# Feed-forward chunks of 384 tokens instead of 256 in the later two thirds of a fused attention and feed-forward kernel

## The chip, the cores and the metric

The kernel runs on one core of a Trainium2 chip. The metric is the device time of one execution in microseconds (us). The kernel before took 922.78 us, the median of three runs (922.3 to 923.05).

## The reference

Eight batches of eight heads, 576 tokens and 64 values per head; all is float32. For each head two attentions are added. One is over tokens averaged in fours (144 of them) and its result is repeated four times. The other is local: a token sees only those less than four positions away, seven at most. The sum is read as 4608 rows of 512 values and goes through a feed-forward layer with a leaky ReLU.

```
q_d, k_d, v_d = means over 4 neighbouring tokens
out = repeat(softmax(q_d k_d^T / 8) v_d, 4) + softmax(q k^T / 8, |i-j| < 4) v
x   = out as (4608, 512)
h   = x @ w_in                       # (512, 2048)
g   = max(h, 0) + alpha * min(h, 0)
y   = g @ w_out                      # (2048, 512)
```

## The kernel before, in words

**Precision.** Weights, x and g are each held as a high and a low part of a four-byte format, so each product of the feed-forward is three matmul groups: high by high, low weight by high operand, high weight by low operand.

**The feed-forward (scope `s`).** The 4608 tokens are 18 chunks of 256 (`T`). A chunk takes 8 steps, 144 in all (`NS`), and a step treats two blocks of 128 of the 2048 hidden values:

- `hidden(s)` (L987): for both blocks 12 matmuls on TensorE (PE): 3 part groups x 4 slices of the 512 inputs, weights 128x128, moving operand x of 256 columns, into one PSUM bank `h` (two of these, 128x512).
- `below(s)` (L993): ScalarE (ACT) writes relu(-h) into the SBUF tile `t`.
- `leak(s)` (L1009): VectorE (DVE) forms t * rise + h, once for each block.
- `split(s)` (L1015): ACT copies the high part `gh`; `spill(s)` (L1021): GpSimd (POOL) subtracts for the low part `gl`. `t`, `gh`, `gl` have two buffers each.
- `product(s)` (L1049): 2 blocks x 3 part groups x 2 output blocks of 128 tokens, 12 matmuls of 512 columns into the two banks `o` of the chunk. The step order on PE is hidden(s), product(s-2), hidden(s+1), product(s-1).
- After a chunk's last step `stage` (L1056) copies each bank `o` to an SBUF tile on ACT and `send` (L1062) writes it out in four transfers on SyncE's queue (SP). `finish_last` does so for the last chunk, with ACT and DVE copies and transfers on both queues.

**The operand of a chunk** is a tile `xx` of 2 (token parity) x 2 (high, low) x 4 x 128 values per partition. There are three buffers, two in pool `two` and one in pool `late`; chunk c takes them in turn (`operand`, `tokens`).

**Attention.** Batch 0 is computed first with matmuls (scopes `p0` to `p3`). From batch 1 on, a *unit* u (3 to 23, `local`) is the local attention of 192 rows of x, so three units make a batch. DVE multiplies keys with the query (`multiply`, L821), sums (`total`, L825), masks (`shift`, L834), normalises (`weights`) and weighs the values (`first`, `weigh`, `gather`, `last`); POOL takes the two farthest keys (`far`, L863). ACT copies the query of each half unit into a PSUM bank first (`scaled`, L815): in most units the first half into bank q and the second into bank l, where the sums also live. In units of `BY_HALF` the two halves run one after the other. Scope `d` (28 of these, four per batch) is the attention over averaged tokens: POOL folds the loads, PE does the matmuls, DVE and ACT the softmax.

When a unit is done, PE transposes it (`flip`, L891), DVE adds the averaged part (`join`, L903, into tile `xf`, one buffer), ACT writes the high operand into `xx` (`place`, L917) and POOL the low one (L208). This happens inside the time of the next unit, in two groups of tokens (`put`).

**The order of the work.** Every action is an event with a time in steps: hidden(s) at s - 1.95, leak(s) at s - 1.15, product(s) at s + 0.6, unit u from `begin[u]` to `begin[u+1]`. `begin` is a table (`UNITS`) and then rises by `U_STEP` = 5.92. Events are issued in the order of their times, and each engine and queue takes its instructions in that order. For the first 42 steps (`HORIZON`) a list written out by hand or by a planner (`ORDER`, 1193 names) replaces the times.

**Weights** are loaded from 0 to some 100 us (`raw`, L289 and L293), and decoded into high and low parts by ACT and DVE.

The changed functions: `tokens`, `spans`, `local`, `hidden`, `below`, `leak`, `split`, `spill`, `product`, `stage`, `send`, `finish_last`, and new ones `third`, `block`, `pieces`, `moving`, `like`.

Of the kernel before, what the change touches and what calls it, by code (L numbers as in the profile page):

```python
# [52 lines left out]
p2.load1 p0.shift0 p0.flip p0.near1 p0.operands p0.near_exps0 p2.load3 p0.shift1 p0.scores p1.turned00 p0.near_exps1
p0.weights i0.convert p1.turn04 p1.turn10 p1.turned04 p1.turned10 i0.bits p1.turn14 p0.load3 p0.over1 p1.turned14
p0.peak o0.convert p1.near0 p1.fold0 p0.exps p1.fold1 o1.load i0.upper p0.invert p2.turn00 i1.load p1.shift0 p1.flip
p0.scaled p0.over0 i0.lower p1.load2 p1.near_exps0 p0.across0 p1.operands p3.load0 o0.bits p0.kept0 p0.across1
p0.held0 p1.near1 p0.kept1 p3.load1 p0.held1 o0.upper p0.over2 p1.shift1 p0.weigh p0.kept2 o0.lower p2.turned00
p0.near_weigh0 d10.load.0 p1.near_exps1 p0.store d10.load.1 p1.weights d10.load.3 p0.near_weigh1 p3.load3 p2.turn10
p0.join0 p2.turn04 p0.high0 p2.turned10 p0.low0 p0.near_weigh2 p2.turned04 p1.scores p2.fold0 p0.join2 p0.join1
i1.convert p2.turn14 p1.load3 p1.peak p1.over0 p2.fold1 p2.turned14 p1.exps p1.over1 p1.fold_v i2.load p2.near1  # L60
i1.bits p2.load2 p1.kept0 p1.kept1 p1.invert p1.over2 o1.convert o2.load p2.near0 i1.upper d10.fold.0 p3.load2
d10.fold.1 p0.high1 p1.scaled p0.low1 d10.load.4 i1.lower p3.turn00 d10.load.2 p1.kept2 p2.flip p3.turned00
# [10 lines left out]
i5.load i4.convert p3.near_weigh1 d10.fold.5 d10.operands p3.near_weigh0 d11.fold.0 d11.load.2 o3.upper d10.scores
d11.load.3 p3.join0 o3.lower p3.high0 p3.low0 p3.near_weigh2 d11.fold.1 s.hidden.0 d10.peak p3.join1 d10.exps
i4.bits d11.load.4 p3.high1 p3.join2 o5.load d10.invert i4.upper p3.low1 change o6a.clear w.load_raw.0.6 d10.scale
i4.lower d11.fold.2 s.hidden.1 w.load_q.3 s.below.0 i5b.convert s.leak.0 i5a.convert i5b.bits d11.fold.4
w.load_kv.3.v s.split.0 d10.turn.0 i5a.bits i5b.upper s.hidden.2 w.load_raw.0.7 s.below.1 d10.turned.0 w.load_kv.3.k
s.leak.1 i5a.upper s.spill.0 o4.convert i5b.lower s.hidden.3 i5a.lower d11.fold.3 s.below.2 o4.bits s.split.1
d11.load.5 s.leak.2 i6a.convert d10.turn.1 s.spill.1 d12.load.0 s.product.0 d10.turned.1 d12.load.1 i6a.bits
o4.upper o6b.clear s.below.3 o4.lower w.load_raw.1.6 i6a.upper i6b.convert s.hidden.4 i6a.lower s.split.2 i6b.bits  # L80
s.spill.2 s.leak.3 i6b.upper w.load_raw.1.6~1 d10.weigh i6b.lower d11.flip i7a.convert s.product.1 d11.operands
i7a.bits i7b.convert i7a.upper i7b.bits o5a.convert s.hidden.5 d11.fold.5 i7a.lower w.load_raw.1.7 s.split.3
i7b.upper o5a.bits s.spill.3 o5b.convert d12.load.2 s.below.4 s.product.2 i7b.lower o5a.upper s.leak.4 o6a.convert
d12.fold.0 o5b.bits s.below.5 o6b.convert s.hidden.6 s.leak.5 s.split.4 d12.fold.1 d12.load.3 o5b.upper o5a.lower
d10.store o5b.lower s.spill.4 o6a.bits s.product.3 d12.fold.2 s.below.6 d12.load.4 s.leak.6 o6a.upper o6b.bits
o7a.clear d11.scores d12.load.5 s.split.5 d12.fold.3 o7a.convert s.product.4 o6a.lower o6b.upper d11.peak o7b.clear
o6b.lower d13.load.0 d11.exps s.spill.5 o7a.bits s.hidden.7 o7b.convert d12.fold.4 s.split.6 d11.invert o7b.bits
d11.scale o7a.upper s.hidden.8 s.below.7 o7a.lower s.spill.6 d13.load.1 o7b.upper s.leak.7 u3.scaled.0
w.place_rest.0 d12.fold.5 o7b.lower u3.multiply.0.0.3 d11.turn.0 u3.scaled.1 d11.turn.1 w.place_rest.1 d11.turned.0
s.product.5 d11.turned.1 s.below.8 u3.multiply.0.3.2 s.leak.8 u3.total.0.3.2 d11.weigh s.split.7 u3.total.0.0.3  # L90
d12.flip d11.store s.spill.7 u3.load_q.4 s.product.6 d12.operands u3.multiply.0.5.2 d13.fold.0 u3.multiply.1.0.3
d13.fold.1 d13.load.2 d12.scores s.split.8 u3.total.0.5.2 d13.load.3 s.spill.8 s.product.7 u3.total.1.0.3 d12.peak
u4.scaled.0 u3.multiply.1.3.2 d13.fold.2 d12.exps s.hidden.9 u3.multiply.1.5.2 d13.load.4 s.stage.0.0 u3.total.1.3.2
s.stage.0.1 d13.load.5 u3.total.1.5.2 s.send.0.1 s.product.8 s.below.9 d13.fold.3 d12.invert u3.shift d12.scale
u3.load_kv.4.k d13.fold.4 s.leak.9 u3.exps u3.weights d12.turn.0 s.split.9 d13.fold.5 d12.turn.1 s.hidden.10
d12.turned.0 d12.turned.1 u3.first.0 u3.far.0 u3.weigh.0.1.3 u3.weigh.0.4.1 u3.gather.0.1.0 s.hidden.11 s.below.10
u3.gather.0.1.1 s.spill.9 s.leak.10 u3.far.1 u3.gather.0.1.2 s.split.10 u3.gather.0.4.0 s.hidden.12 s.below.11
u3.weigh.1.1.3 u3.weigh.1.4.1 s.spill.10 s.leak.11 d20.load.0 s.product.9 d20.load.1 u3.last.0 d20.load.2 s.below.12
u3.first.1 s.leak.12 u3.gather.1.1.0 d13.flip s.split.11 s.product.10 u3.gather.1.1.1 d13.operands s.spill.11
u3.gather.1.1.2 d20.fold.0 u3.gather.1.4.0 u4.multiply.0.0.3 d20.fold.1 d12.weigh s.split.12 d13.scores d12.store  # L100
u4.multiply.0.3.2 s.spill.12 s.product.11 u4.total.0.0.3 u3.load_kv.4.v d13.peak d20.load.3 u4.multiply.0.5.2
d13.exps s.hidden.13 d20.fold.2 u3.last.1 u4.total.0.5.2 d20.load.4 u4.scaled.1 d13.invert u4.total.0.3.2 d13.scale
u4.load_q.5 s.product.12 u4.multiply.1.0.3 s.below.13 s.send.0.0 d20.fold.3 u4.multiply.1.3.2 u4.total.1.0.3
d20.fold.4 d13.turn.0 d20.load.5 d13.turn.1 d13.turned.0 s.hidden.14 u4.total.1.3.2 d13.turned.1 d21.load.0
u4.multiply.1.5.2 s.leak.13 u4.total.1.5.2 d13.weigh s.split.13 u4.load_kv.5.k d20.fold.5 u3.flip.0 s.below.14
u4.shift d13.store s.hidden.15 s.leak.14 s.spill.13 u4.exps u3.join.0 s.split.14 s.spill.14 u4.weights u3.place.0.0
u3.flip.1 d20.flip s.below.15 u3.place.0.1 u4.weigh.0.1.3 s.product.13 d20.operands d21.fold.0 u4.weigh.0.4.1
u3.join.1 u4.far.0 s.leak.15 u3.place.1.0 d20.scores d21.load.1 u4.first.0 s.split.15 s.product.14 d20.peak
d21.load.2 u4.gather.0.1.0 d20.exps d21.load.3 u3.place.1.1 u4.gather.0.1.1 u4.gather.0.1.2 s.spill.15 d20.invert
u4.weigh.1.1.3 s.hidden.16 d20.scale u4.far.1 u4.gather.0.4.0 u4.last.0 u4.weigh.1.4.1 s.product.15 s.below.16  # L110
u4.first.1 d21.fold.1 s.leak.16 u4.load_kv.5.v u4.gather.1.1.0 d21.fold.2 s.split.16 d21.load.4 u4.gather.1.1.1
# [1137 lines left out]
```

## Time and profile before

| | |
|---|---|
| median of three runs | 922.78 us |
| the profiled execution | 925.19 us, span 923.4 us |
| PE busy | 900.0 us (97%) |
| DVE busy | 774.3 us (84%) |
| POOL busy | 543.5 us (59%) |
| ACT busy | 420.7 us (46%) |
| granted TensorE clock, mean | 0.975 |
| moved to and from memory | 98.27 MB |

The page shows one execution. The span runs from the first instruction to the last; the profiled execution's own time also holds what lies around it, 1.8 us. Busy time of PE counts a matmul to its modelled end, so that overlapping matmuls look like one long piece; how far the starts lie apart says how fast they go. Lines are grouped by the source line, engine, operation and tiles; after the bar stands the idle time of the engine just before these instructions and what ended it. In the slices a digit is the busy share in tenths of one fortieth of the span, 23.1 us. `h` is the bank of the hidden values, `o` the output bank, `xx` the operand, `wih`, `wil`, `woh`, `wol` the high and low weights.

### The profile page before, as it was taken

To read this page: it belongs to the slowest core of one execution; us is meant where nothing else is said; L and a number is where in the kernel's file an instruction comes from. 1 tells how busy PE (TensorE), PEld (TensorE's weight loads), DVE (VectorE), ACT (ScalarE), POOL (GpSimd) and SP (SyncE) were. 2 spreads that over 40 slices of the span, in tenths; PEclk is the share of its full clock that TensorE was granted. 3 is DMA by queue.
4 is the path that set the end of the run, shared out by engine and by line. 5 is a ranking of instruction groups with operands and counts; after the bars stand their busy time and mean duration, and the time that the engine had idled before them with its cause. 6 is when DMAs were issued, how large, how long until landed. Compare 5 with 4: busy or idle time off the path is not lost.

```text
span 923.4 us, 17740 instructions
## 1 busy us (share of the span) xinstructions
PE 900.0 (97%) x6474; PEld 828.2 (90%) x6474; DVE 774.3 (84%) x1387; ACT 420.7 (46%) x1061; POOL 543.5 (59%) x683
## 2 busy tenths in 40 slices
PE   6799999999999999999999999999999999999998
PEld 5579999999988999999999999999999999999997
DVE  5787899999999499889999889899998899996111
ACT  4798854544444444344444444344444452233221
POOL 2126775886486665748767566867757753426221
PEclk9757999999999999999999999999999999999999
DMA  8997533334334113333133234233334222211000
GB/s 186 220 308 267 175 108 126 104 100 119 114 109 131 60 54 112 97 119 113 61 115 123 79 102 128 72 115 123 85 114 125 65 76 70 74 35 25 1 23 23
DMA packets 63195, 98.27 MB, mean 106 GB/s; under 512 B 23556, under 2 KB 28932, under 8 KB 63108
## 3 DMA queue, kind: packets, MB, share of 16 engines
q1 hardware_dynamic: 62916, 96.88, 35.3%
q8 instruction: 51, 0.84, 0.4%
q10 hardware_dynamic: 192, 0.26, 0.1%
q14 instruction: 36, 0.29, 0.1%
HBM read 87.67 MB, written 9.44 MB: 105 GB/s over the span
## 4 chain that ended last, share of the span: by engine, by line
PE 77%; DVE 12%; DMA 3%; SPq 2%; ACT 2%; issue 1%; POOL 1%; ACTq 0%; DVEq 0%; POOLq 0%
PE h L987 35%; PE o L1049 34%; DMA raw<-in_moe_w_in 3%; DVE qk L821 3%; DVE ls L825 2%; PE s L409 2%; DVE t L1009 2%; PE pv L443 2%; SPq L513 2%; DVE lb L882 2%; DVE pv L879 1%; PE pT L433 1%; PE xp L891 1%; PE qkT L396 1%; DVE xf L903 1%
## 5 line engine op out<-in xcount | busy, mean ns | idle before, releaser
L987 PE MATMUL h<-xx,wih 128*128 128x256 f32 x2304 | 332.6, 278 | 1.6 <-DVE t L1009 1.6
L1021 POOL TENSOR_TENSOR gl<-t,gh 128x512 fp32r<-128x512 f32 x142 | 182.1, 1282 | 241.6 <-ACT gh L1015 227.4
L987 PEld LDWEIGHTS h<-xx,wih 128*128 128x128 f32 x2304 | 299.0, 193 | 8.1 <-DVE t L1009 1.2
L1009 DVE SCALAR_TENSOR_TENSOR t<-t,rise,h 128x256 f32<-128x256 f32 x288 | 124.7, 474 | 73.6 <-ACT t L993 73.2
L1049 PE MATMUL o<-woh,gh 128*128 128x512 f32 x576 | 184.5, 391 | 0.5 <-ACT sg L1056 0.5
L1049 PE MATMUL o<-woh,gl 128*128 128x512 f32 x576 | 177.7, 379 | 0.0
L1049 PE MATMUL o<-wol,gh 128*128 128x512 f32 x576 | 177.7, 379 | 0.0
L987 PE MATMUL h<-xx,wil 128*128 128x256 f32 x1152 | 176.4, 276 | 0.0
L1015 ACT CAST gh<-t 128x512 fp32r<-128x512 f32 x144 | 89.5, 621 | 177.8 <-PE o L1049 88.9
L387 POOL TENSOR_TENSOR ld<-ld 72x256 f32<-72x256 f32 x167 | 125.4, 751 | 69.3 <-DMA ld<-in_q 35.0
L993 ACT ACTIVATE t<-h 128x512 f32<-128x512 f32 x144 | 86.0, 597 | 160.6 <-PE h L987 128.3
L987 PEld LDWEIGHTS h<-xx,wil 128*128 128x128 f32 x1152 | 152.4, 193 | 0.0
L825 DVE TENSOR_REDUCE ls<-qk 128x12 f32<-128x768 f32 (+1 forms) x126 | 135.4, 1081 | 2.3
L1049 PEld LDWEIGHTS o<-woh,gl 128*128 128x128 f32 x576 | 109.1, 189 | 15.3
L1049 PEld LDWEIGHTS o<-wol,gh 128*128 128x128 f32 x576 | 109.1, 189 | 14.8
L1049 PEld LDWEIGHTS o<-woh,gh 128*128 128x128 f32 x576 | 99.8, 190 | 11.2 <-issue 2.2
L882 DVE TENSOR_TENSOR lb<-lb,pv 128x384 f32<-128x384 f32 x168 | 94.7, 564 | 4.5
L821 DVE TENSOR_TENSOR qk<-k,qp 128x768 f32<-128x768 f32 (+1 forms) x78 | 83.3, 1076 | 5.0 <-ACT qp L815 5.0
L879 DVE TENSOR_TENSOR pv<-v,lb 128x1152 f32<-128x1152 f32 x84 | 79.3, 952 | 2.3
L821 DVE TENSOR_TENSOR qk<-k,lb 128x768 f32<-128x768 f32 (+1 forms) x48 | 51.5, 1078 | 1.5 <-ACT lb L815 1.5
L208 POOL TENSOR_TENSOR xx<-xf,xx 128x256 fp32r<-128x256 f32 (+3 forms) x47 | 43.7, 936 | 13.8 <-ACT xx L917 13.8
L903 DVE TENSOR_TENSOR xf<-xp,od 128x128 f32<-128x128 f32 (+3 forms) x110 | 40.0, 415 | 7.5 <-PE xp L891 5.0
(146 smaller groups left out, 997.2 us busy)
## 6 DMA issues: line engine op xcount, KB each, us to landing
v<-in_v SPq DMA_DIRECT2D x41, 384.0 KB
k<-in_k SPq DMA_DIRECT2D x41, 384.0 KB
out<-sg SPq DMA_DIRECT2D x140, 64.0 KB
raw<-in_moe_w_in SPq DMA_DIRECT2D x16, 512.0 KB
raw<-in_moe_w_out SPq DMA_DIRECT2D x16, 512.0 KB
ld<-in_q SPq DMA_DIRECT2D x56, 144.0 KB
ld<-in_k SPq DMA_DIRECT2D x56, 144.0 KB
ld<-in_v SPq DMA_DIRECT2D x56, 144.0 KB
```

Source lines behind the costliest of these rows:

```text
L387: e.tensor_tensor(lv[:, :, 0:128], lv[:, :, 0:128], lv[:, :, 128:256], op=ALU.add)
L821: nc.vector.tensor_tensor(st["qk", half, d0][:, :nd], window(tiles[u, "k"], half, d0, nd), st["qp", half].unsqueeze(1).to_broadcast([128, ...
L825: nc.vector.tensor_reduce(out=st["s"][:, half, d0:d0 + nd, :].rearrange("p a b -> p (a b)"), in_=st.pop(("qk", half, d0))[:, :nd].rearrang ...
L879: nc.vector.tensor_tensor(st["pv", half, d0][:, :nd], window4(tiles[u, "v"], half, d0, nd), prob(half, d0, nd), op=ALU.mult)
L882: nc.vector.tensor_tensor(st["acc"], st["acc"], st["pv", half, d0][:, i], op=ALU.add)
L903: nc.vector.tensor_tensor(xf.rearrange("p a t (s e) -> p e t a s", e=2)[:, par, k0:k0 + nk], tp.rearrange("p (t s e a) -> p e t a s", t=4, ...
L987: nc.tensor.matmul(ph[:, j], w[:, m, 128 * o:128 * o + 128], x[:, part, m], start=(i == 0), stop=(i == 11))
L993: nc.scalar.activation(t, hs[st], AF.Relu, scale=-1.0)
L1009: nc.vector.scalar_tensor_tensor(t[:, j], t[:, j], rise[:, f:f + 1], h[:, j], op0=ALU.mult, op1=ALU.add)
L1015: nc.scalar.copy(gh, t)
L1021: (nc.vector if f"s{st}.split" in ON_VECTOR else nc.gpsimd).tensor_tensor(gl, t, f32(gh), op=ALU.subtract)
L1049: nc.tensor.matmul(outs[c][m], g[:, j, 128 * m:128 * m + 128], wo[w][n][:, :, o].rearrange("p e a -> p a e"), start=(f == 0 and i == 0), s ...
```

## The change

The first six chunks (`SMALL`, 48 steps) stay as they are. The other 3072 tokens become eight chunks of 384. Such a chunk takes 16 steps of one block of 128 hidden values each, with a `PACE` of 0.75 of an old step: 12 matmuls of 384 columns into the first 384 columns of a bank `h`, elementwise work on 128x384, and 9 output matmuls (3 part groups x 3 output blocks). There are 48 + 128 = 176 steps on the same time scale of 144. `leak`, `split` and `spill` are planned 0.2 of a step later.

A chunk's operand takes one and a half of the three old buffers (`A`, `B`, `C`; C has 384 values more): even large chunks use all of A and the first three blocks of B, odd ones all of C and the last two blocks of B, as `pieces` lists. High and low parts are blocks of 192 values per parity, so a low part is written with two or three instructions where it was one.

The third output block uses PSUM bank q (`bank("q", ...)`) and is staged through the tile of the joins, `xf`. So from unit 11 on (`SINGLE`) attention leaves bank q alone: the query is copied to bank l only, first one half and later the other, and the very first multiply of a unit reads the query in SBUF. Outputs of large chunks leave in transfers of up to 128 rows, the first block's on ACT's queue. Units 13, 17 and 21 are no longer done by halves, `UNITS` goes up to 12 with units 9 to 12 earlier than before, then `U_STEP` is 5.96, and the second join of odd units from 9 on comes earlier. The written-out order is a new one of 1507 names, up to step 56, which also orders the first 48 steps anew. The branch of `below` and `leak` for POOL, which was not in use, goes.

```diff
+SMALL = 6
+SIZES = [256] * SMALL + [384] * ((B * S - 256 * SMALL) // 384)
+STARTS = [sum(SIZES[:c]) for c in range(len(SIZES))]
+STEPS = [(c, f, 2 if n == 256 else 1) for c, n in enumerate(SIZES) for f in range(0, NF, 2 if n == 256 else 1)]
+PACE = [1.0 if n == 2 else 0.75 for _, _, n in STEPS]
+WHEN = [sum(PACE[:s]) for s in range(len(STEPS))]
+SINGLE = 11
-UNITS = {3: 7.5, 4: 12.2, 5: 17.07, 6: 22.7, 7: 28.0}
-U_STEP = 5.92
-BY_HALF = (5, 9, 13, 17, 21)
+UNITS = {3: 7.5, 4: 12.2, 5: 17.07, 6: 22.7, 7: 28.0, 8: 33.8, 9: 39.1, 10: 44.4, 11: 50.0, 12: 55.6}
+U_STEP = 5.96
+BY_HALF = (5, 9)
-HORIZON = 42
+HORIZON = 56
...
+    def third(name):
+        if name not in shared:
+            shared[name] = (late if name == "C" else two).tile([128, 2432 if name == "C" else 2048], F32R, tag="xx", name=f"xx{name}")
+        return shared[name]
+
+    def block(name, k, n=1):
+        if k == 5:
+            return third(name)[:, 2048:2432].rearrange("p (m e a) -> p m e a", m=1, e=2)
+        return third(name)[:, 0:2048].rearrange("p (e x) -> p e x", e=2)[:, :, 192 * k:192 * (k + n)]             .rearrange("p e (m a) -> p m e a", m=n)
+
+    def pieces(c, i):
+        if c % 2 == 0:
+            return (("A", 0, 0, 4),) if i == 0 else (("A", 4, 0, 1), ("B", 0, 1, 4))
+        return (("C", 0, 0, 4),) if i == 0 else (("C", 4, 0, 1), ("C", 5, 1, 2), ("B", 3, 2, 4))
+
+    def moving(c, i, m):
+        if c < SMALL:
+            return xT[c].rearrange("p e i m a -> p i m a e")[:, i, m]
+        (x, k), = ((x, f + m - a) for x, f, a, z in pieces(c - SMALL, i) if a <= m < z)
+        return block(x, k)[:, 0].rearrange("p e a -> p a e")
...
+                if single:
+                    st["qp", 0] = st["qp", 1] = lb[:, 0:384].rearrange("p (h n) -> p h n", h=2)
...
+            if single and (half, d0) == (0, 0):
+                q_ = tiles[u, "q"][:, :, 0:3, :].rearrange("p h t d -> p h (t d)")
+            else:
+                q_ = st["qp", half]
...
-                hi, lo = (tokens(c, i, o, n) for i in range(2))
+                    for ms, lo in tokens(c, 1, o, n):
+                        sub(lo, pairs(src[:, ms]), f32(hi[:, :, ms]))
...
+        c, f0, nf = STEPS[st]
+        nm = SIZES[c] // 128
+        if f0 == 0:
+            outs[c] = [ps_o.tile([128, DM], F32, tag="po", name=f"o{c}_{m}") if m < 2 else bank("q", f"o{c}_{m}")
+                       for m in range(nm)]
...
+        if m < 2:
+            sg = two.tile([128, DM], F32, tag="stage", name=f"sg{c}_{m}", bufs=SB)
+        else:
+            sg = late.tile([128, DM], F32, tag="xf", name=f"sg{c}_{m}")
...
+        if c >= SMALL:
+            o = 0
+            for n, ap in rows(STARTS[c] + 128 * m, 128):
+                (nc.scalar if m == 0 else nc.sync).dma_start(ap, sg[o:o + n, :])
+                o += n
+            return
...
+        slip = 0.2 * (nf == 1)
+        at(t - (1.15 - slip) * p, leak, s)
+        at(t - (1.0 - slip) * p, split, s)
+        at(t - (0.99 - slip) * p, spill, s)
...
-            t = when["before 0"] + 0.25 if u == 4 else when["before 1"]
+            t = when["before 0"] + (0.25 if u == 4 else 0.8) if u == 4 or u % 2 == 0 and u > 9 else when["before 1"]
```

More of the change, by code (lines that the diff above doesn't have):

```diff
@@ L53 @@
[L53 to L62, printed above, removed]
@@ L73 @@
[L73 to L82, printed above, removed]
@@ L83 @@
[L83 to L111, printed above, removed]
-s.hidden.17 s.stage.1.0 s.spill.16 u4.gather.1.1.2 d21.load.5 s.stage.1.1 s.send.1.0 u4.gather.1.4.0 d21.fold.3
@@ L133 @@
-u6.multiply.1.5.2 d30.fold.1 u6.total.1.5.2 d30.fold.2 u6.shift s.hidden.27 s.split.24 s.spill.24 u6.exps u6.weights
-s.below.26 u6.far.0 u6.weigh.0.1.3 s.product.23 s.leak.26 u6.first.0 u6.load_kv.7.k u6.weigh.0.4.1 u6.far.1
-d22.weigh s.split.25 u6.gather.0.1.0 d23.scores s.stage.2.0 s.spill.25 d22.store s.stage.2.1 s.hidden.28 d23.peak
-s.below.27 u6.gather.0.1.1 u7.scaled.0 s.leak.27 d23.exps u6.gather.0.1.2 s.product.24 u6.gather.0.4.0
-u6.weigh.1.1.3 s.send.2.1 u6.weigh.1.4.1 s.hidden.29 s.split.26 u6.last.0 d30.load.3 d23.invert s.spill.26
@@ L168 @@
-d40.load.2 s.stage.4.1 s.send.4.0 u9.scaled.0 u9.multiply.0.0.3 s.product.40 s.below.41 u9.multiply.0.3.2
-u9.total.0.0.3 d33.flip s.leak.41 d32.weigh d33.operands d40.fold.0 s.send.4.1 u9.multiply.0.5.2 s.hidden.42
-s.split.41 u9.total.0.3.2 d32.store s.spill.41 u9.scaled.1 u9.total.0.5.2 u9.load_q.10 u9.shift u8.flip.0 s.below.42
-d33.scores u9.exps u8.join.0 s.hidden.43 s.leak.42 u8.place.0.0 d33.peak u8.place.0.1 d40.load.3 s.split.42
-u9.weights d33.exps u8.flip.1 u9.first.0 s.spill.42 s.product.41 u8.join.1 s.below.43 d33.invert u9.far.0
@@ new lines @@
+s.split.7 d11.turn.1 s.product.6 d11.turned.0 s.spill.7 u3.total.0.5.2 d11.turned.1 u3.total.1.0.3 d13.load.2
+s.below.9 u3.multiply.1.3.2 d11.weigh s.split.8 d12.flip u3.multiply.1.5.2 d11.store s.spill.8 s.product.7
+d12.operands u3.total.1.3.2 u3.load_kv.4.k u4.scaled.0 d13.fold.0 u3.total.1.5.2 d13.fold.2 s.leak.9 d13.load.3
+d12.scores s.stage.0.0 u3.shift d13.fold.1 s.stage.0.1 s.hidden.10 s.split.9 d12.peak u3.exps d12.exps s.spill.9
+u3.weights u3.first.0 u3.far.0 u3.weigh.0.1.3 d13.load.4 s.product.8 s.below.10 d13.load.5 d12.invert u3.weigh.0.4.1
@@ new lines @@
+u5.shift s.hidden.19 s.split.17 u4.join.0 d21.fold.5 d22.load.1 u5.exps s.split.18 u5.weights d22.fold.0
+u4.place.0.0 d22.load.2 u5.first.0 d20.weigh s.spill.17 u5.weigh.0.1.3 d22.load.3 d21.scores d20.store u4.place.0.1
+u4.flip.1 s.below.19 u5.weigh.0.4.1 s.hidden.20 d21.peak s.leak.19 u5.far.0 d21.exps u4.join.1 u5.gather.0.1.0
+u4.place.1.0 s.hidden.21 d21.invert u5.gather.0.1.1 d21.scale u4.place.1.1 u5.gather.0.1.2 d22.fold.2
+u5.gather.0.4.0 u5.multiply.1.0.3 s.product.17 d22.fold.1 u5.last.0 d22.fold.3 u5.total.1.0.3 d22.load.4 d22.load.5
@@ new lines @@
+s.stage.3.0 s.stage.3.1 u6.place.1.1 u7.last.1 d30.turn.1 s.split.33 s.hidden.34 u8.total.0.3.2 s.spill.32
+d30.turned.0 d32.load.1 d30.turned.1 u8.scaled.1 u8.total.0.0.3 s.spill.33 d32.load.2 u8.multiply.0.5.2
+u7.load_kv.8.v d31.flip s.below.34 d30.weigh d32.fold.0 u8.multiply.1.0.3 d31.operands s.hidden.35 d30.store
+d32.fold.1 u8.total.0.5.2 d32.fold.2 s.leak.34 u8.total.1.0.3 d31.scores s.below.35 d32.load.3 u7.flip.0 d31.peak
+s.hidden.36 u7.join.0 d32.load.4 d31.exps d32.load.5 s.leak.35 u7.place.0.0 d31.invert u8.multiply.1.3.2 s.send.3.1
@@ new lines @@
+d33.flip u9.multiply.0.0.3 d32.weigh d33.operands s.spill.38 s.product.37 s.below.39 d40.load.2 u9.multiply.0.3.2
+d32.store d40.fold.0 s.below.40 s.leak.39 d40.fold.1 d40.load.3 s.leak.40 s.hidden.41 s.split.39 u9.total.0.3.2
+d40.load.4 s.spill.39 u9.total.0.0.3 d40.fold.2 s.product.38 u9.multiply.0.5.2 s.below.41 d40.fold.3 s.leak.41
+u9.scaled.1 u9.total.0.5.2 u8.flip.0 s.split.40 u9.shift d33.scores u8.join.0 u9.exps s.spill.40 s.product.39
+d33.peak u8.place.0.0 u9.weights d33.exps u8.place.0.1 u9.weigh.0.1.3 u8.flip.1 s.stage.4.0 s.hidden.42 u9.far.0
@@ new lines @@
+d33.invert u9.first.0 s.split.41 u9.load_q.10 u8.join.1 s.stage.4.1 d33.scale u9.gather.0.1.0 u9.weigh.0.4.1
+u8.place.1.0 u9.gather.0.1.1 s.spill.41 s.product.40 s.below.42 u9.gather.0.1.2 s.leak.42 u8.place.1.1
+u9.multiply.1.0.3 d40.fold.4 s.send.4.1 d33.turn.0 s.split.42 u9.gather.0.4.0 s.spill.42 u9.total.1.0.3 d33.turn.1
+d33.turned.0 s.hidden.43 d33.turned.1 d40.load.5 u9.last.0 u9.multiply.1.3.2 s.send.4.0 u9.multiply.1.5.2 d33.weigh
+s.below.43 u9.total.1.3.2 s.product.41 u10.scaled.0 d40.fold.5 d33.store u9.total.1.5.2 s.leak.43 u9.shift~1
@@ new lines @@
+u9.flip.0 s.split.43 u9.load_kv.10.k d40.flip u9.join.0 u9.exps~1 s.product.42 s.spill.43 d40.operands u9.weights~1
+u9.place.0.0 u9.place.0.1 u9.first.1 u9.weigh.1.1.3 s.hidden.44 u9.far.1 u9.weigh.1.4.1 u9.gather.1.1.0
+u9.gather.1.1.1 u9.gather.1.1.2 s.product.43 s.below.44 u9.gather.1.4.0 s.leak.44 d41.load.0 u9.last.1 d41.load.1
+s.split.44 d41.load.2 u10.scaled.1 d40.scores s.spill.44 u9.load_kv.10.v u9.flip.1 d40.peak s.hidden.45 u9.join.1
+u10.load_q.11 d40.exps u10.multiply.0.0.3 u9.place.1.0 d41.fold.0 s.hidden.46 s.below.45 u10.multiply.0.3.2
@@ L174 @@
+d43.load.4 u12.scaled.0 s.hidden.59 s.below.58 d43.load.5 d43.fold.3 s.leak.58 s.split.58 u11.load_kv.12.v
+s.spill.58 s.hidden.60 s.below.59 s.leak.59 d43.fold.4 s.product.58 s.split.59 d42.weigh s.spill.59 s.below.60
+u11.flip.0
 """.split()
```

323 lines of the change are left out of this document (196 added, 127 removed).

## The prediction

> **What bounds the kernel now.** I read the page first (busy shares, then the slices, then the costliest groups), then the chain of waits over the last 40 us, then the table by stage and the timelines of single places.
>
> ```profile
> span 923.4 us, 17740 instructions
> PE 900.0 (97%) x6474; PEld 828.2 (90%) x6474; DVE 774.3 (84%) x1387; ACT 420.7 (46%) x1061; POOL 543.5 (59%) x683
> ...
> PE   6799999999999999999999999999999999999998
> ...
> DVE  5787899999999499889999889899998899996111
> ...
> PEclk9757999999999999999999999999999999999999
> ...
> L987 PE MATMUL h<-xx,wih 128*128 128x256 f32 x2304 | 332.6, 278 | 1.6 <-DVE t L1009 1.6
> ...
> L1049 PE MATMUL o<-woh,gh 128*128 128x512 f32 x576 | 184.5, 391 | 0.5 <-ACT sg L1056 0.5
> ```
>
> TensorE is full from the fourth slice to the last, and the two matmul lines waited about 2 us in the whole run. A busy PE is not yet a PE at its rate, so I looked at how far starts lie apart near the end, in the chain of waits (start, length, what):
>
> ```profile
> 75.05 7.35 PE h L987 x48
> ...
> 903.54 2.68 PE h L987 x24
> 906.22 2.59 PE o L1049 x12
> 908.81 2.68 PE h L987 x24
> ```
>
> One step is 908.81 - 903.54 = 5.27 us: 24 matmuls of 256 columns in 2.68 us, 111.7 ns each, and 12 of 512 columns in 2.59 us, 215.8 ns each. The chain holds them end to end with no gap. So the time is the start (the first h at 75.05 us), plus what TensorE must issue, plus few waits. Work on the other engines counts only where it makes TensorE wait.
>
> ```profile
> 360.00:644.00 284.00, 284.00 (x2039) 263.48 (x2037) 261.23 (x465) 124.26 (x326) 194.03 (x247) 1.00 0.34 104
> ```
>
> The columns after PE and PEld are DVE, ACT and POOL. In the stage that the change rebuilds DVE works 261.23 of 284 us (92%), POOL 68%, ACT 44%; DVE is the second engine, with 8% to spare.
>
> **The change, part by part.** *Fewer, wider h matmuls.* The last 3072 tokens were 12 chunks x 8 steps x 24 = 2304 matmuls of 256 columns; they become 8 chunks x 16 steps x 12 = 1536 of 384. The columns streamed are the same; what goes is the fixed share of 768 matmuls. The trace has no 384. Below: three quarters of the 512's 215.8 is 161.9 ns. Above: one and a half 256's is 167.6 ns. Between, on the line through both widths, (111.7 + 215.8)/2 = 163.75 ns. I take the line, since 384 lies midway. Before 2304 x 111.7 = 257.4 us, after 1536 x 163.75 = 251.5 us: **-5.9 us** (bounds -8.7 and 0). The o matmuls stay 1728 of 512 columns, only in groups of 9.
>
> [...]
>
> *Elementwise work by the step.* 96 steps of 512 elements become 128 of 384.
>
> ```profile
> 600.42 0.86 DVE L1009 SCALAR_TENSOR_TENSOR t<-t,rise,h 128x256 f32<-128x256 f32 x2
> ```
> ```profile
> L355 DVE SCALAR_TENSOR_TENSOR wol<-temp,woh 128x512 fp32r<-128x512 f32 x16 | 11.2, 727 | 5.5 <-ACT woh L349 5.5
> ```
> ```profile
> L1021 POOL TENSOR_TENSOR gl<-t,gh 128x512 fp32r<-128x512 f32 x142 | 182.1, 1282 | 241.6 <-ACT gh L1015 227.4
> ...
> L1015 ACT CAST gh<-t 128x512 fp32r<-128x512 f32 x144 | 89.5, 621 | 177.8 <-PE o L1049 88.9
> ...
> L993 ACT ACTIVATE t<-h 128x512 f32<-128x512 f32 x144 | 86.0, 597 | 160.6 <-PE h L987 128.3
> ```
> ```profile
> L815 ACT COPY qp<-q 128x384 f32<-128x384 f32 x26 | 12.7, 487 | 0.7 <-DVE qk L821 0.7
> ...
> L208 POOL TENSOR_TENSOR xx<-xf,xx 128x384 fp32r<-128x384 f32 x5 | 5.1, 1027 | 0.7 <-ACT xx L917 0.7
> ```
>
> DVE's leak: two of 256 cost 0.86 us; a 384 midway between 0.43 and 0.73 is 0.58, so 128 x 0.58 = 74 us for 96 x 0.86 = 83: 8 us less. POOL's subtraction: 1.03 us by the row of 384 elements, 128 x 1.03 = 132 for 96 x 1.28 = 123 us. ACT: a 384 copy takes 0.49, so 128 x 2 x 0.49 = 125 for 96 x (0.62 + 0.60) = 117 us. All of it lies under TensorE, by 8% on DVE, 32% on POOL, 56% on ACT. Without that cover POOL's and ACT's 17 us would count and DVE's 8 would be won.
>
> *A shorter window to hide it in.* Each step may lag until the step after next needs its PSUM bank.
>
> ```profile
> 595.99 2.68 PE h L987 x24
> ...
> 608.01 2.68 PE h L987 x24
> ```
>
> The h of 595.99 ended at 598.67, its leak at 601.28, and the bank is asked for at 608.01: 6.7 us to spare. The way from there has two o groups and one h group; with the small steps it is 2 x 0.65 + 0.7 = 2.0 us shorter, and the leak is planned 0.2 step (0.8 us) later: 3.9 us remain. Cost 0 here; if DVE lags by more than that, each step pays.
>
> *Attention pulled forward and single scaled bank.* Bank q is freed for the third output block, so from unit 11 on the scaled query is copied twice into bank l, and the first multiply of a unit reads q from SBUF. That multiply now has two SBUF inputs while POOL works. The nearest rows are the mask additions, which also have two, against a line of the same shape whose other input lies in PSUM:
>
> ```profile
> L834 DVE TENSOR_TENSOR ls<-ls,mask_r x9: 194/245/1676, 185.0 to 829.1; 128x84 f32<-128x84 f32 x5, 128x42 f32<-128x42 f32 x4
> ```
> ```profile
> L834 DVE TENSOR_TENSOR ls<-ls,mask_r 128x84 f32<-128x84 f32 x5 | 2.7, 537 | 0.1
> ...
> L836 DVE TENSOR_TENSOR ls<-ls,lb 128x84 f32<-128x84 f32 x16 | 3.9, 242 | 0.6
> ```
>
> 537 - 242 = 0.3 us more on average, at worst 1676 - 242 = 1.4 us. Thirteen multiplies: 4 us of DVE, at most 19, below the 8% of some 390 us, 31 us. Queued behind a stretched multiply is the next leak, and behind that TensorE; the 3.9 us above hold one such stretch. Cost 0.
>
> [...]
>
> The units up to 12 start earlier (every 5.45 steps from unit 8 to 12 instead of 5.92). DVE works 0.92 x 5.92 = 5.45 steps' time per unit, so it is just full there, as it is in the unbroken slices of nines from 115 to 300 us, which the matmul lines passed with the 2 us of waits that they have in all. I put **+0.5 us** (0 to +4). The re-ordered first 48 steps hold the same work with nearly the same loads ahead of the first h matmul; that start hangs on transfers:
>
> ```profile
> 16.51 3.14 SPq L513
> ...
> 49.12 10.77 DMA raw<-in_moe_w_in
> ```
>
> Two loads of w_in (i0, i1) move a few places up SP's queue, past query and key loads; the rest of the queue keeps its content. The first h follows the decoding of the weights that this 10.77 us transfer brings; a load put ahead or behind shifts it by about the longest issue there, 3.14 us (an estimate): bounds -3 and +3 us, value 0. Three units fewer by halves save DVE some small instructions, hidden.
>
> *Outputs and the end.* A chunk now has three staging copies of some 0.6 us (512 elements, as ACT's rows above), the third in the tile of the joins, and sends of 128 rows, one from ACT's queue behind its own copy, ahead of the other two copies. TensorE reaches the next use of the second block a 1.95 us h group and three o matmuls later, which covers it. At the end the third block's copy is ACT's second, and starts behind three matmuls (0.65 us) instead of six; two sends of the second block stand ahead of it on SP: **+0.3 us** (0 to +1).
>
> *Sum:* -5.9 + 0.5 + 0.3 = -5.1 us. The profiled execution took 925.19 us (span 923.4 and 1.8 around it), so it would take 920.1; the median of the runs is 922.78, 2.4 below it, so **917.7 us**.
>
> **Rivals.**
>
> *Faster than the sum* (14%): the 384 costs its lower bound, 161.9 ns (-8.7), and the start moves up to 3 us: 922.8 - 8.7 - 3 + 0.8 = 911.9 us. For it: the 512's small fixed share; against: the start waits for as many bytes as before.
>
> *The operand comes late* (12%, slower): a chunk of 384 is two whole units, so its h matmuls wait for the second unit's low half; with 256 the last unit was often needed only in part.
>
> ```profile
> 447.06 0.68 DVE L903 TENSOR_TENSOR xf<-xp,od 128x128 f32<-128x128 f32 x2
> ```
> ```profile
> 452.56 0.75 POOL L208 TENSOR_TENSOR xx<-xf,xx 128x256 fp32r<-128x256 f32 x1
> ```
>
> From this join to the end of its low half passed 6.3 us. In the new plan the join of unit 11 stands at step 57.4 (55.6 + 1.8), chunk 7's first h at 58.5: 1.1 steps of 5.9 us and the 8 matmuls that need only the high half, 7.8 us. From 8 us after the join on TensorE waits, at up to seven chunk starts. Lateness of 10 us gives 7 x 2.2 = 15 us: 922.8 - 5.1 + 15 = 933 us. For it: little room; against: the second join now stands ahead of the unit's POOL products, behind which the one shown waited, and the room grows by 0.08 steps per chunk.
>
> *Columns are all that counts* (6%): 167.6 ns per 384, no gain: 922.8 + 0.8 = 923.6 us. Against it: 215.8 is less than twice 111.7.
>
> *The gain is given back in the new order* (6%): DVE, full from unit 3 to 12, makes TensorE wait 5 us in the steps up to 60: 922.8 - 5.1 + 4.6 = 922.3 us.
>
> **How the numbers follow.** The forecast holds 62%, from 914.5 to 920.5 by its own terms. A measurement of this kernel tells 0.2% (1.8 us) from no change. Faster: the forecast and the first rival, with a little of the last, 77%. Slower: the late operand and parts of the last two, 15%; within 0.2%: 8%. The range 911.5 to 923.5 leaves out the late operand (12%) and a corner below.
>
> **What would show it.** Right: the h groups of 12 about 163.75 x 12 = 1.97 us long and 3.9 us apart near the end; TensorE waiting under 3 us on the two matmul lines; the first h near 75 us. Wrong: h waiting on POOL's xx at chunk starts, or on DVE's t in mid-stage; groups of 12 at 2.01 us (no gain); the first h elsewhere than 72 to 78 us; qk multiplies of 1152 elements at 2 us with TensorE waiting behind them.

## The result: slower by one per cent

The changed kernel takes 933.36 us (median of 6 runs, 930.85 to 934.78), the kernel before 923.67 us beside it (6 runs, 922.3 to 925.85). The ratio is 1.0103, with a 95% interval of 1.0084 to 1.0122. The forecast was 917.7 us, in a range of 911.5 to 923.5. The profiled executions took 925.19 us before and 930.85 us after. The first lies above its median and the second is the fastest of its six, so the two traces show 5.7 us of the 9.7 us between the medians. The rest is taken for scatter from run to run, which these two traces cannot show.

The page of the profile of the changed kernel, the span, the slices and two groups of matmuls:

```profile
span 929.0 us, 16176 instructions
...
PE 895.3 (96%) x5706; PEld 817.6 (88%) x5706; DVE 761.0 (82%) x1297; ACT 430.8 (46%) x1118; POOL 556.1 (60%) x759
...
PE   6889999999999999999999999999999999999994
...
PEclk9968999999999999999999999999999999999998
...
L1126 PE MATMUL o<-woh,gl 128*128 128x512 f32 x576 | 168.6, 380 | 2.1 <-POOL gl L1096 2.1
...
L1067 PE MATMUL h<-xx,wih 128*128 128x256 f32 x768 | 110.9, 279 | 2.2 <-DVE t L1084 1.9
```

TensorE works 4.7 us less than before, yet the span is 5.6 us longer. Its last slice is a 4 where it was an 8: the kernel goes on after TensorE has stopped. The last o matmul starts at 915.83 us (918.88 before), 3.05 us earlier, and the end of the span follows 13.2 us later (4.5 before).

The end of the chain of waits (start, length, what):

```profile
900.65 1.95 PE h L1067 x12
902.60 1.94 PE o L1126 x9
904.54 1.95 PE h L1067 x12
...
910.38 5.84 PE o L1126 x27
916.23 0.02 issue
916.25 0.58 ACT sg L1160
```

A step is 904.54 - 900.65 = 3.89 us, and twelve matmuls of 384 columns take 1.95 us, 162.5 ns each. The forecast's own sign for a right step has come, and a little better than it said (1.97 us and 3.9 us). Its sign for the waits has not: TensorE waited 4.7 us on the two matmul lines, not under 3. Even so, most of the loss is not there: the chain ends with the last staging copy at 916.83 us, and the span at 929.0 us: 12.2 us in which no engine computes. The kernel before had 3.4 us there (copy over at 919.99, span 923.4).

What runs in that time are the last transfers to the output. The DMA view of the window from 917 to 929 us, in 40 slices of 0.3 us, first of the changed kernel:

```profile
GB/s 34 7 14 7 48 55 61 143 123 178 287 219 116 143 178 82 55 34 34 48 48 55 48 55 48 55 48 55 48 55 48 55 34 27 27 7 0 0 0 0
DMA packets 449, 0.77 MB, mean 64 GB/s; under 512 B 72, under 2 KB 72, under 8 KB 449
...
out<-sg SPq DMA_DIRECT2D x1, 128.0 KB
```

and the same window of the kernel before:

```profile
GB/s 0 0 0 0 0 0 0 0 198 219 301 157 55 212 212 335 62 0 0 0 0 0 0 0 0 0 0 0 0 0 0 0 0 0 0 0 0 0 0 0
DMA packets 384, 0.52 MB, mean 44 GB/s; under 512 B 128, under 2 KB 128, under 8 KB 384
...
out<-sg SPq DMA_DIRECT2D x4, 64.0 KB
...
out<-sg ACTq DMA_DIRECT2D x4, 64.0 KB
```

The kernel before writes its 0.52 MB in 2.6 us, some 200 GB/s on average. The changed kernel has 116 to 287 GB/s for 2.4 us, while the small pieces of its third block are moved too, and then trickles at 34 to 55 GB/s from 921.8 to 926.9 us. A packet of 2 KB takes 84 ns in the trace (the median of the large pieces' packets), 24 GB/s for one lane (one of the core's 16 DMA engines) that moves packet after packet. So 50 GB/s are two lanes. The trace's busy share says the same: from 922 to 926.5 us the 16 engines are busy 0.13 of the time on average, which is 2.1 of them. From 917 to 919 us, with the first large piece under way, it is 0.25, which is 4, and in the kernel before 0.80 from 919.4 to 922 us, which is 12.8. The large pieces that the change introduced have destinations whose outermost dimension counts 4 (128 rows) or 2 (64 rows); in the pieces of 32 rows the first dimension of more than one element counts 32. The trace does not name a packet's engine, but the count of packets under 512 B goes with those counts too: 128 for the eight small pieces of the kernel before, 16 each, and 72 here, where four small pieces would leave 8 for the three large ones, which fits 4 + 2 + 2. A large piece of 128 rows on ACT's queue at 442 us has 4 of them among its 132 packets. The two pieces of 64 rows, 32 packets of 84 ns on each of two lanes, take 5.4 us one after the other, about the length of the trickle; on lanes of their own they would take half of it. That the outer count sets the number of lanes, and that both pieces of 64 rows go on the same two, is an estimate from these numbers.

The costs that the forecast took from neighbouring rows, as the changed kernel's groups by shape show them:

```profile
L1096 POOL TENSOR_TENSOR gl<-t,gh 128x384 fp32r<-128x384 f32 x128 | 128.5, 1005 | 165.4 <-ACT gh L1090 93.5 <-PE o L1126 62.4 <-PE h L1067 9.0
...
L1084 DVE SCALAR_TENSOR_TENSOR t<-t,rise,h 128x384 f32<-128x384 f32 x128 | 78.0, 609 | 77.1 <-ACT t L1078 76.9
...
L896 DVE TENSOR_TENSOR qk<-k,q 128x1152 f32<-128x1152 f32 x13 | 18.7, 1442 | 0.0
```

The subtraction costs 1005 ns (1.03 us forecast), the leak 609 (0.58), and the first multiply with the query in SBUF 1442 on average, 0.1 us more than the same shape from PSUM (1346); most take 1.35 us, and the longest 2123 ns. None of them comes near the loss.

The waits of TensorE, POOL and DVE from 350 to 920 us (in total, times, longest), in the changed kernel:

```profile
PE o L1126 <- POOL gl L1096: 2.1, 3, 1.1
```
```profile
POOL ld L428 <- DMA ld<-in_v: 13.0, 2, 6.9
...
POOL ld L428 <- DMA ld<-in_k: 9.5, 3, 8.0
```
```profile
DVE xf L978 <- DMA out<-sg: 11.6, 5, 3.2
```

and POOL's one wait for a load in the kernel before:

```profile
POOL ld L387 <- DMA ld<-in_v: 1.0, 1, 1.0
```

Waits for transfers have come up on POOL and DVE, and one on TensorE, which hangs on POOL. How, the chain shows between 514 and 531 us:

```profile
514.61 1.00 POOL gl L1096
515.62 0.69 POOL ld L428
516.86 10.88 DMA ld<-in_v
527.82 0.73 POOL ld L428
529.09 0.97 POOL gl L1096
530.10 0.91 PE o L1126 x3
```

and SP's timeline just before it:

```profile
513.96 2.68 SPq L1144 DMA_DIRECT2D out<-sg  x3
516.86 3.01 SPq L418 DMA_DIRECT2D ld<-in_v  x2
```

SP issues three large sends, and then two loads of values. These land only after 10.9 us. POOL stands at the addition that needs them, and the gl that TensorE waits for stands behind it on POOL. The same happens at 586.67 us (a load of keys, 11.40 us).

### The profile page after: what moved, and what is told of

Same layout as the page of the kernel before. It is cut to its first block, busy times and chain, and to the rows that moved or that the text cites. A ratio compares the mean times of both kernels' runs of the same rounds, so it can differ in the third digit from the quotient of the medians.

```text
span 929.0 us, 16176 instructions
## 1 busy us (share of the span) xinstructions
PE 895.3 (96%) x5706; PEld 817.6 (88%) x5706; DVE 761.0 (82%) x1297; ACT 430.8 (46%) x1118; POOL 556.1 (60%) x759
## 3 DMA queue, kind: packets, MB, share of 16 engines
q10 hardware_dynamic: 1020, 1.97, 0.9%
## 4 chain that ended last, share of the span: by engine, by line
PE 73%; DVE 13%; DMA 6%; ACT 2%; issue 2%; POOL 2%; SPq 1%; ACTq 0%; DVEq 0%; POOLq 0%
PE h L1067 33%; PE o L1126 33%; DMA ld<-in_v 3%; DVE lb L957 2%; DVE ls L900 2%; DVE pv L954 2%; PE s L450 2%; DMA ld<-in_k 1%; DVE t L1084 1%; PE pv L484 1%; DVE qk L896 1%; PE xp L966 1%; PE pT L474 1%; DMA fv<-in_v 1%; DVE xf L978 1%
## 5 line engine op out<-in xcount | busy, mean ns | idle before, releaser
L1096 POOL TENSOR_TENSOR gl<-t,gh 128x384 fp32r<-128x384 f32 (+1 forms) x174 | 188.5, 1085 | 215.8 <-ACT gh L1090 142.9
L1084 DVE SCALAR_TENSOR_TENSOR t<-t,rise,h 128x384 f32<-128x384 f32 (+1 forms) x224 | 119.3, 551 | 82.7 <-ACT t L1078 82.4
L1078 ACT ACTIVATE t<-h 128x384 f32<-128x384 f32 (+1 forms) x176 | 91.4, 519 | 176.7 <-PE h L1067 146.9
L1090 ACT CAST gh<-t 128x384 fp32r<-128x384 f32 (+1 forms) x176 | 95.4, 542 | 137.7 <-DVE t L1084 72.1
L1067 PE MATMUL h<-xx,wih 128*128 128x256 f32 x768 | 110.9, 279 | 2.2 <-DVE t L1084 1.9
L1067 PEld LDWEIGHTS h<-xx,wih 128*128 128x128 f32 x768 | 98.8, 193 | 5.0 <-issue 1.6
L1067 PE MATMUL h<-xxC,wih 128*128 128x384 f32 x384 | 84.9, 330 | 0.0
L1067 PE MATMUL h<-xxA,wih 128*128 128x384 f32 x320 | 74.6, 331 | 0.0
L1067 PE MATMUL h<-xxB,wih 128*128 128x384 f32 x320 | 72.9, 326 | 0.0
L1067 PE MATMUL h<-xx,wil 128*128 128x256 f32 x384 | 59.0, 277 | 0.0
```

The source lines that it names most:

```text
L1067: nc.tensor.matmul(ph[:, j], w[:, m, 128 * o:128 * o + 128], moving(c, part, m), start=(i == 0), stop=(i == 11))
L1078: nc.scalar.activation(t, hs[st], AF.Relu, scale=-1.0)
L1084: nc.vector.scalar_tensor_tensor(t[:, j], t[:, j], rise[:, f0 + j:f0 + j + 1], h[:, j], op0=ALU.mult, op1=ALU.add)
L1090: nc.scalar.copy(gh, t)
L1096: (nc.vector if f"s{st}.split" in ON_VECTOR else nc.gpsimd).tensor_tensor(gl, t, f32(gh), op=ALU.subtract)
```

## The experiments

Theory A: the large pieces are moved by few lanes, and that makes the end late; in the middle the same lanes hold up loads and joins. Against it stood B (TensorE's own waits are the loss), C (the size or the queue of the pieces), and for the middle several mechanisms, named below. Each kernel was timed against the kernel before on the same chip. For the experiments on the middle (all small pieces, one half each, all on ACT's queue) the diff shows the edit there alone; their end goes in pieces of 32 rows, as in the first experiment.

**The end mended.** The last chunk's blocks go out in pieces of 32 rows by turns on both queues:

```diff
-            if m < 2:
-                o = 0
-                for n, ap in rows(STARTS[c] + 128 * m, 128):
-                    nc.sync.dma_start(ap, sg[o:o + n, :])
-                    o += n
-                continue
             for i in range(4):
                 (_, ap), = rows(STARTS[c] + 128 * m + 32 * i, 32)
```

> The changed kernel with one edit: the last chunk's first two blocks are sent as the kernel before sends its own, in pieces of 32 rows, by turns on SP's and ACT's queue, instead of one piece of 128 and two of 64 rows each on SP. Theory A (few lanes): a piece whose destination has 4 or 2 outer rows is moved two to four packets at a time; the end of the changed profile shows it (last staging copy over at 916.8, last packet at 927.7, about 50 GB/s in between, where the kernel before needs 3.4 us from its last copy to its end). Then the span ends 3 to 4 us after the last copy instead of 12.2: 8 to 9 us are won, 933.4 becomes about 924.6, ratio to the kernel before 0.998 to 1.004. Theory B (TensorE's waits are the loss, the end is only where it shows): 932 to 934, ratio about 1.009.

Measured: 924.61 us, ratio 0.9997 (0.9984 to 1.001). That is 8.75 us below the changed kernel, as A has it. Its transfers from 917 to 929 us, in the same slices:

```profile
GB/s 0 0 109 219 253 273 294 178 294 130 68 219 225 314 48 0 0 0 0 0 0 0 0 0 0 0 0 0 0 0 0 0 0 0 0 0 0 0 0 0
```

The trickle is gone; the last copy is over at 919.36 and the span at 922.8 us. B falls for the end.

**Large pieces, dimensions exchanged.** The same pieces, bytes, queue and output rows as in the changed kernel, but the destination counts 32 outermost (rows change places within a piece, which alters these rows of the output):

```diff
-                    nc.sync.dma_start(ap, sg[o:o + n, :])
+                    nc.sync.dma_start(bass.AP(ap.tensor, ap.offset, [ap.ap[1], ap.ap[0], ap.ap[2]]), sg[o:o + n, :])
```

> The changed kernel, the last chunk's first two blocks still in pieces of 128 and 64 rows on SP, with the same bytes to the same rows of the output, but the two outer dimensions of the destination exchanged (32 outer by 4 or 2 inner instead of 4 or 2 by 32; this permutes rows within a piece, so these rows of the output are not the reference's). Theory A (the count of the outer dimension sets how many packets move at a time): like the pieces of 32 rows, 924 to 926.5, ratio 1.000 to 1.004, the last packet 3 to 5 us after the last copy. [...] Theory C (the size of the pieces, or that they stand on one queue, makes the end late): 931 to 934, ratio 1.008 or more, the last packet 9 us or more after the last copy.

Measured: 924.36 us, ratio 0.9995 (0.9984 to 1.0007). The DMA view of the same window:

```profile
GB/s 0 0 0 89 389 369 239 191 198 280 321 273 273 0 0 0 0 0 0 0 0 0 0 0 0 0 0 0 0 0 0 0 0 0 0 0 0 0 0 0
...
out<-sg SPq DMA_DIRECT2D x2, 128.0 KB
```

Neither the size nor the queue was at fault. The order of two dimensions alone decides at the end, 924.36 us against 933.36.

**The same end in the kernel before.**

```diff
-            for i in range(4):
-                (_, ap), = rows(T * c + 128 * m + 32 * i, 32)
-                (nc.sync if i % 2 == 0 else nc.scalar).dma_start(ap, sg[32 * i:32 * i + 32, :])
+            o = 0
+            for n, ap in rows(T * c + 128 * m, 128):
+                nc.sync.dma_start(ap, sg[o:o + n, :])
+                o += n
```

> The kernel before with one edit, the change's own one: the last chunk's two blocks are sent as one piece of 128 rows and two of 64 (destination 4 or 2 outer by 32) on SP's queue. Theory A: the two slowest lanes carry 32 + 32 + 32 rows of some 84 ns (the packets of such pieces in the changed profile), 8.1 us, where the pieces of 32 rows are done 2 us after the last copy: 5 to 8 us slower, 929 to 932, ratio 1.005 to 1.009. Theory B (TensorE's waits): no change, 923 to 925, ratio 1.000 within 0.002.

Measured: 932.11 us, ratio 1.0079 (1.0066 to 1.0092), 7.2 us slower than the kernel before at 924.87. Its transfers from 917 to 931 us, in slices of 0.35 us:

```profile
GB/s 0 0 0 0 0 0 0 0 0 0 23 18 12 12 47 47 59 53 35 76 47 64 82 82 94 99 94 105 94 70 59 47 47 59 47 29 0 0 0 0
DMA packets 264, 0.52 MB, mean 37 GB/s; under 512 B 8, under 2 KB 8, under 8 KB 264
```

The three large pieces have 8 packets under 512 B here too, and never pass 105 GB/s. This one edit, alone, costs most of what the whole change lost.

**All outputs in pieces of 32 rows,** in the middle too:

```diff
-        if c >= SMALL:
-            o = 0
-            for n, ap in rows(STARTS[c] + 128 * m, 128):
-                (nc.scalar if m == 0 else nc.sync).dma_start(ap, sg[o:o + n, :])
-                o += n
-            return
         for i in range(4):
```

> The changed kernel with every output, in the middle and at the end, sent in pieces of 32 rows, as the kernel before does (the middle ones all on SP). Theory A with D (the joins that waited for the third block's slow send, 11.6 us of DVE's idle time in the changed profile, delay DVE, then ACT and POOL, and are behind TensorE's waits for POOL's gl of 2.8 us): 2 to 3 us below the kernel with the mended end alone, about 922, ratio 0.995 to 1.001, no waits of joins for a send and few of TensorE for gl. Theory A without D (POOL is late by its own work): within 1 us of the kernel with the mended end, TensorE still waits 2 us and more for gl. Theory B: 932 and more.

Measured: 919.93 us, ratio 0.9944 (0.9932 to 0.9956): faster than both kernels, and 4.7 us below the one with the mended end, more than either theory gave. POOL's waits for loads from 350 to 920 us:

```profile
POOL ld L428 <- DMA ld<-in_v: 2.9, 2, 2.0
...
POOL ld L428 <- DMA ld<-in_k: 1.2, 1, 1.2
```

They fall from 22.5 to 4.1 us; no join waits for a send any more, and TensorE no more for gl. Of the 4.7 us, TensorE's listed waits after 350 us show 2.3: 2.1 us for gl and 0.4 for the leak with the mended end, against 0.2 in all here. Its weight loads (gl is loaded as the weights) wait for gl as well, 3.7 us from 350 to 850 us in the changed kernel; part of that lies under running matmuls, as PEld and PE are busy for 817.6 and 895.3 us of the same 929.0. How the rest of the 4.7 us comes about is not shown. From the first h to the start of the last o pass 836.85 us, against 841.00 in the changed kernel and 843.90 in the kernel before.

**One half of the middle each.** D1 blamed the joins, which wait for the third block's send because it leaves from their tile; D2 the loads behind large sends. First only the third block in small pieces, then only the first two:

```diff
-        if c >= SMALL:
+        if c >= SMALL and m < 2:
```

> The changed kernel with the mended end (924.6 us), and in the middle only the third block of each chunk sent in pieces of 32 rows; the first goes on as one or two large pieces from ACT, the second from SP. All small in the middle gave 919.9. Theory D1 (the joins wait for the third block's send, 8.8 us of DVE's time, as its tile is theirs): the whole 4.7 us, 919.5 to 921, and DVE waits no more for a send. Theory D2 (the loads of queries, keys and values that are issued behind large sends come late; POOL waited 22.5 us for them in the changed kernel, 4.1 us with all small, and its gl behind them was what TensorE waited for): only the part that the third block's pieces hold up, 921.5 to 924, and POOL still waits more than 8 us for loads.

```diff
-        if c >= SMALL:
+        if c >= SMALL and m == 2:
```

> The other half: the changed kernel with the mended end, in the middle the first and second block in pieces of 32 rows (on SP) and the third in large ones. Theory D1: nothing won, 924 to 925.5, the joins wait for the send as before. Theory D2: 2 to 4 us won, 920.5 to 922.5, POOL's wait for loads falls below 12 us.

Measured: 921.14 us (0.9959, 0.9945 to 0.9973) and 921.15 us (0.9958, 0.9941 to 0.9975). With the third block small, POOL and DVE still wait in the middle:

```profile
POOL ld L428 <- DMA ld<-in_v: 9.3, 2, 5.0
...
POOL ld L428 <- DMA ld<-in_k: 7.1, 3, 5.7
```
```profile
DVE xf L978 <- DMA out<-sg: 2.1, 2, 1.3
```

With the third block large the joins wait 0.8 us and POOL 14.3 us for loads. In neither does TensorE wait for gl after 350 us. So neither D1 nor D2 holds as put: each half alone brings three quarters of the gain or more, they do not add, and the first run's 16.4 us of POOL's waits cost TensorE nothing. (By the medians it is three quarters, but the intervals of the ratios overlap with that of all small pieces; in the traces the stretch from the first h to the last o is 836.88 and 837.18 us, as good as the 836.85 there.) An account that fits, but that no run shows directly: the large pieces of one chunk add up on the same lanes, and with fewer of them the delay stays within the room that the schedule has.

**All large pieces on ACT's queue,** none ahead of the loads on SP's:

```diff
-                (nc.scalar if m == 0 else nc.sync).dma_start(ap, sg[o:o + n, :])
+                nc.scalar.dma_start(ap, sg[o:o + n, :])
```

> The changed kernel with the mended end; in the middle all three blocks in large pieces, as in the changed kernel, but all issued from ACT's queue, so that no load stands behind a send on its own queue (the loads are all on SP's). Theory Q (the loads wait behind the sends in SP's queue): POOL's waits for loads fall from 22.5 to about 4 us, and with them TensorE's 2 us of waits for gl; the joins still wait for the third send; 921 to 923. Theory L (loads and sends share the few DMA lanes that large pieces use, whichever queue they came from): POOL still waits more than 10 us, 924 to 926; ACT's longer issues add up to 1 us. [...]

Measured: 929.43 us, ratio 1.0049 (1.003 to 1.0069), 4.8 us slower than with the mended end, which no theory foresaw. POOL's wait for loads is down from 22.5 to 1.5 us, as Q has it: the loads had been held up by the large sends ahead of them on their own queue. But the loss has moved. TensorE's longest waits from 100 to 920 us:

```profile
PE h L1067 <- DVE t L1084: 4.3, 5, 1.5
PE o L1126 <- POOL gl L1096: 1.2, 1, 1.2
PE o L1126 <- ACT sg L1137: 0.8, 1, 0.8
```

Of the 4.3 us for the leak, 2.7 lie after 350 us, where the kernel with the mended end has 0.4. The joins wait 6.8 us for sends, which now follow one another on one queue, and ACT issues 28 pieces of 0.57 us between its copies. Which of the two weighs more stays open.

**The new order alone.** The kernel before, with the first 44 steps in the changed kernel's order, units 8 and 9 at its times, unit 10 at 45.0 (44.4 there, 45.76 before), and units 13, 17 and 21 no longer by halves:

```diff
-UNITS = {3: 7.5, 4: 12.2, 5: 17.07, 6: 22.7, 7: 28.0}
+UNITS = {3: 7.5, 4: 12.2, 5: 17.07, 6: 22.7, 7: 28.0, 8: 33.8, 9: 39.1, 10: 45.0}
-BY_HALF = (5, 9, 13, 17, 21)
+BY_HALF = (5, 9)
 HORIZON = 42
 ORDER = """
-p0.load0 clear masks p0.load1 p0.load2 p1.load0 p1.load1 p0.turn00 p0.turn04 i0.load p0.turned00 p0.fold0
+p0.load0 masks p0.load1 clear p0.load2 p1.load0 i0.load p0.turn00 p1.load1 p0.turn04 p0.turned00 p0.fold0
...
```

> The kernel before (chunks of 256 throughout, 32-row pieces, scaled query through the banks) with the first 44 steps in the changed kernel's written-out order and the units 8 to 10 at its earlier times. Theory O (the new order costs TensorE waits in the first steps: the profiles have waits of 200 ns and more that sum to 4.3 us before, from 100 us to 350 us, in the new one, against 2.5 us): 1.5 to 3 us slower than the kernel before, ratio 1.0015 to 1.003. Rival (the order costs nothing of its own; the start varies by as much between runs): ratio 0.999 to 1.001.

Measured: 926.93 us, ratio 1.0024 (1.0008 to 1.004), 2.2 us slower, a price of all these edits together. Then the other way round: all outputs in small pieces, and the old order up to the h matmuls of step 30, with what is left of the new one behind it:

```diff
 ORDER = """
-p0.load0 masks p0.load1 clear p0.load2 p1.load0 i0.load p0.turn00 p1.load1 p0.turn04 p0.turned00 p0.fold0
+p0.load0 clear masks p0.load1 p0.load2 p1.load0 p1.load1 p0.turn00 p0.turn04 i0.load p0.turned00 p0.fold0
...
```

> The changed kernel with all outputs in pieces of 32 rows (919.9 us), and the written-out order of the kernel before for everything that stands there ahead of the h matmuls of step 30; what is left follows in the changed kernel's order. Theory O (the new order costs TensorE's waits in the early steps, 2.2 us measured alone in the kernel before): the waits of TensorE between 189 and 250 us fall from some 2.7 us to about 1, 1 to 2.5 us won, 917.5 to 919, ratio 0.992 to 0.9935. Rival (that difference was the start's scatter from run to run, 75 to 79 us for the first h): 919.5 to 920.5, ratio 0.9938 or more, and the time from the first h to the last o, 836.9 us before, is not shorter.

Measured: 919.17 us, ratio 0.9947 (0.9932 to 0.9963), the same as with the new order throughout. The time from the first h to the last o is 837.03 us, not shorter. In the first kernel the order with its edits has a price, in the second the old order brings nothing that could be measured; what the order costs the changed kernel stays open between 0 and 2 us.

**All large pieces with dimensions exchanged,** in the middle (shown) and at the end, as in the second experiment (the rows change places in the middle as well):

```diff
-                (nc.scalar if m == 0 else nc.sync).dma_start(ap, sg[o:o + n, :])
+                (nc.scalar if m == 0 else nc.sync).dma_start(bass.AP(ap.tensor, ap.offset, [ap.ap[1], ap.ap[0], ap.ap[2]]), sg[o:o + n, :])
```

> The changed kernel with all its large pieces, from the same queues as there, but with the two outer dimensions of the destination exchanged for each, in the middle too (the same bytes to the same rows, permuted within a piece, so the rows of the output from the seventh chunk on are not the reference's). Theory A (the lanes, not the size or the queue, are what costs in the middle as at the end): joins wait under 1 us for sends and POOL under 6 us for loads, TensorE's waits after 350 us under 1 us; 919 to 921.5, like the kernel with all pieces small, ratio 0.993 to 0.9965. Theory C (large pieces, one of them on ACT's queue, hold up the loads behind them): 923 to 925, as with the mended end alone, POOL waits some 20 us for loads.

Measured: 920.52 us, ratio 0.9963 (0.9948 to 0.9978). No wait of POOL for these loads nor of a join for a send is left after 350 us, so in the middle too the order of the two dimensions decides.

**The change's middle sends in the kernel before:**

```diff
+        if c >= 6:
+            o = 0
+            for n, ap in rows(T * c + 128 * m, 128):
+                (nc.scalar if m == 0 else nc.sync).dma_start(ap, sg[o:o + n, :])
+                o += n
+            return
         for i in range(4):
```

> The kernel before with the other half of the change's sends: from its seventh chunk (of 256) on, the first block goes in large pieces from ACT and the second from SP, as in the changed kernel; the last chunk still in pieces of 32 rows. Theory E (the lanes' hold-up costs only where the schedule has no room: two blocks per 47 us, and no third in the joins' tile): POOL waits longer for loads (more than 5 us, 1.0 before), but TensorE under 1 us more; ratio 0.999 to 1.002. Rival F (a large piece costs by itself, whatever the chunk, as the middle sends cost the changed kernel 4.7 us): 2 to 5 us slower, ratio 1.002 to 1.0055.

Measured: 924.19 us, ratio 0.9998 (0.9987 to 1.001). POOL's waits for loads and TensorE's only wait, both after 350 us:

```profile
POOL ld L387 <- DMA ld<-in_v: 9.4, 3, 4.3
```
```profile
PE o L1049 <- ACT sg L1056: 0.5, 1, 0.5
```

The loads come late here too, POOL waits for them nine times as long as before, and nobody pays: theory E. The middle sends cost 4.7 us in the changed schedule, with three blocks per chunk, and nothing that could be measured in the old one, with two. Whether the third block, its tile or the shorter steps make the difference is not separated.

## Why the prediction was wrong

*Fewer, wider h matmuls:* right in kind, its size too small. 384 columns take 162.5 ns where the line between the two known widths gave 163.75: 257.4 - 1536 x 162.5 ns = -7.8 us instead of -5.9. The measured value lies nearer to three quarters of the 512's, 161.9 ns, which the prediction had as its lower bound.

*Outputs and the end:* the step that failed, "+0.3 us (0 to +1)". It counted copies, matmuls and issues, and took it that a piece of 128 rows moves as the four pieces of 32 do. The end cost 8.75 us in the changed kernel and 7.2 alone. Of the middle it said that TensorE's time to the next use of a block "covers it"; it looked at the blocks' banks, not at the loads behind the sends and the joins in the third block's tile. That cost 4.7 us. In place of the +0.3 us the runs show 13.4 us for the form of the sends, 8.75 at the end and 4.7 in the middle.

*Sum:* without these two the same kernel stands at 919.93 us against 924.87, -4.9 us, where the sum was -5.1. It is right there in part by luck. In the traces the stretch from the first h to the last o is 7.05 us shorter than before, and the end from there 1.2 us longer (914.31 to 920.0, against 918.88 to 923.4), as three blocks have to be copied and sent where there were two: the matmuls were put too small and the mended end too cheap.

*Rest of the steps:* elementwise work, the shorter window and the scaled query cost nothing measurable, as forecast. "+0.5 (0 to +4)" for a full DVE is not refuted; the order's price lies in it. The first h came at 74.83 us (74.98).

*Rivals:* "the operand comes late" gave 933 us, and the time came out at 933.36, but by another mechanism: TensorE waited 0.3 us in all on an operand, not 15. The number does not confirm it. "Columns are all that counts" fell with 162.5 ns. "Given back in the new order" has a measured 2.2 us in the kernel before, and none that could be shown in the changed one. None of the rivals had the transfers' lanes, and the range, built from the rivals, could not hold them.

## What to carry to other kernels

When a change alters a transfer, read how the outer dimensions of its destination are ordered, not only its bytes and its issue: fewer, larger pieces were slower by 9 us at the end of this kernel, and exchanging two dimensions made them as fast as the small ones (924.36 us against 924.61). The end of this kernel had no cover: what stood behind the last copy, 12.2 us against 3.4 before, counted in full (8.75 us were won with the end mended). In the middle a slow transfer cost this kernel nothing in the old schedule and 4.7 us in the new one, and there taking away either half of the large pieces was nearly enough.
